# A fused attention and two-layer MoE kernel: TensorE carries the attention state on for three units instead of five, and every due offset of the planner is another

## The chip, the cores and the metric

The kernel runs on one core of a Trainium2 chip. Five engines work beside each other, each on its own list of instructions in a fixed order, and they wait for each other by semaphores: TensorE (PE in the profile; PEld is its weight loads) multiplies matrices, VectorE (DVE) and ScalarE (ACT) do elementwise work, GpSimd (POOL) too, and SyncE (SP) issues the transfers. The metric is the device time of one execution in microseconds (us).

## The reference

Three parts follow each other. The first is a recurrent attention over 4 batches, 8 heads, 768 steps and head size 48:

```python
for t in range(S):
    kt, vt, rt = (k[:, :, t], v[:, :, t], r[:, :, t])
    cur = np.einsum('bhd,bhe->bhde', u[None] * kt, vt)
    y[:, :, t] = np.einsum('bhd,bhde->bhe', rt, state + cur)
    state = w[None, :, :, None] * state + np.einsum('bhd,bhe->bhde', kt, vt)
```

Its output, 3072 tokens of 384 numbers, goes through a dense layer pair (384 to 2048 to 384, with a piecewise quadratic between). The third part picks one of eight experts for each token and applies that expert's pair of matrices (384 to 1024 to 384, relu), scaled by the gate.

## The kernel before

**Attention.** The 768 steps of a batch are cut into six units of 128 steps, so there are 24 units, u0 to u23. A unit is a few small TensorE jobs with work of the other engines between:

- `rk` (line 541, DVE) scales r and k of the unit by powers of the decay. Its input comes by a DMA into one of four buffers.
- `s0` (616, later 624, PE) makes the two 128-step score tiles of all heads; `e0` and `e1` (636, DVE) mask them out of PSUM.
- `dp` (579, PE) makes the diagonal terms from `kr` (573, POOL); `dvp` (605, DVE) multiplies them into v. From the fifth unit on this goes by `ru0`, `ru1` (566, 568, POOL), a reduction `dg2` (589, DVE) and `dv` (605, POOL).
- `s1` (694 and 690, PE) makes the unit's output; it reads dv, the masked scores and the state that the unit before left. `s3h` (748, ACT) and `s3l` (754, DVE) split the output into a rounded part xh and the rest xl.
- `s2` (PE) adds the unit's keys times values to the state. There are two ways, and `by_pe(u)`, that is `u < BY_PE` (line 674), picks one. By TensorE: one matmul with the identity brings the old state (128x384, line 715) into PSUM and eight matmuls of 48x48 (720) add to it, and ScalarE scales the sum into the new state in four instructions (680). By VectorE: sixteen smaller matmuls (724) make only the new part, VectorE adds the old state in two instructions (735; 737 where a batch begins), and ScalarE scales that in four (743).

**First layer.** Groups of nine matmuls `h` (lines 341 to 343, three products of rounded parts and rests) make 128 hidden features for 512 tokens. The first four groups, k0 to k3, take 256 tokens each: k0 and k1 need the outputs of u0 and u1. ScalarE does `relu`, `over` and `sqr` (835, 839, 842), VectorE `max` (845), ScalarE `gh` (849), GpSimd `gl` (854), and six matmuls `o` (876, 877) with three more `og` (879) add the features to the output. Before that, each 768-column piece of the weights, which come as 64-bit numbers, is put together on VectorE: pieces w0 and w1 with `wp1` to `wp3` and `wlp` (439, 442, 445, 461, two instructions each), the others with `wb1` to `wb3` (417, 420, 423) and `wlo` on POOL (481). Piece w0 is the first of the input matrix (k0 needs it), w1 the first of the output matrix, w2 the second of the input matrix; w2 is loaded first, and w1 and w0 later.

**Second layer.** It has the same shape with other names (psm, psh2, o2) and follows when the first is done.

**What sets the order.** Nothing of this order is written by hand. Each job above is a task with an engine, a planned duration, the tasks it needs, the buffers it takes and a due time. `Schedule.run` (line 111) goes through planned time, and of the tasks that could start first on an engine it takes the one with the smallest due time. To each due time, `Schedule.add` adds up to three numbers of the table `SHIFT` (line 239), found by the kind of task, by the unit or step, and by both together. The engines' instructions are then recorded in the planned order, so that table is the order. Where TensorE is planned to be idle before the first `o`, `keep_warm` (line 759) records matmuls on constants, called fillers here, of 128x128 as many as fit the planned gap (line 1719); they write a PSUM tile that nobody reads.

Two things off the path matter here. `wkr` (line 670, ACT) overwrites the second half of the table wk and so waits until `kk` (550, POOL) has read it for u2 to u7; `kk` of a unit reads that unit's keys in natural order (attn), which SP loads. And the four buffers for the units' inputs come free only with the unit's `s1`: the input of u7 waits for the end of `s1` of u3, and SP, which issues in order, issues the natural keys of u7 behind it.

Of the kernel before, what the change touches and what calls it, by code (L numbers as in the profile page):

```python
# [234 lines left out]
def d_pe(n):  # L235
    return n / 2300 + 0.011


SHIFT = {"": 31.25, "az": 14, "b0": -19.75, "b1": -26, "b2": 4.5, "b3": 22.75, "b4": -30.5, "b5": 295.25, "dd":
# [15 lines left out]
         "le0": -5.75, "le1": -39.25, "le2": -6.75, "lka": 9.25, "lkl": -20.5, "lkm": -9.5, "look": -248.5, "max":  # L255
# [14 lines left out]
         46.25, "sm": 330, "sma": -190, "smc0": -63.25, "smc1": 0.25, "sqa": -87.25, "sqs": -32.25, "swd": -3.5,  # L270
# [8 lines left out]
         "whp": 6.5, "wkc": -2.75, "wkd": -3.25, "wkr": 6.75, "wl": 109.75, "wlo": 201.5, "wlp": -72.5, "wp1": 25.25,  # L279
         "wp2": 35.25, "wp3": 54.5, "x1ld": 28.75, "x2h": 30.5, "x2l": 36, "x2ld": -14.25, "xth0": -21, "xth1": 8,  # L280
         "xtl0": -57.75, "xtl1": -6.25, "xts0": -46.5, "xts1": -3.5, "xts2": -54.75, "xts3": 7.25, "z": 98.5, "zs":
         -119.75}
U_DVE, U_PE, W_DVE = 4.7, 3.5, 4.0
ON_DVE = {}
KK_PE, W_PSUM, G_PSUM, DV_PSUM, BY_PE = 2, 2, 0, 4, 5


@with_exitstack
def fused_kernel(ctx, tc, att, wcol, wrow, ub, ucol, win, wout, emb, tau, w1, w2, out):
# [987 lines left out]
    def m2_store(b, i, o):  # L1277
# [5 lines left out]
                    "a": 2, "gh": 3, "gl": 3, "ru": 1, "dg": 2, "dv": 1, "at0": 1, "at1": 1, "state": 2, "kk": 2, "hw": 2, "gate": 1},  # L1283
                   {"PE": 5.5, "DVE": 5.75, "Pool": 4.4, "ACT": 2.2, "SP": 1.73}, SHIFT)
    parts = ((0, 0, 6), (1, 0, 8), (0, 6, NF), (1, 8, NF))
# [668 lines left out]
```

## Time and profile before

| what | value |
|---|---|
| median of 3 runs | 710.27 us (709.94 to 710.44) |
| the profiled execution | 710.95 us |
| its span, from the first to the last instruction | 709.1 us |
| TensorE busy | 699.4 us (99%) |
| VectorE busy | 450.4 us (64%) |
| ScalarE busy | 416.7 us (59%) |
| GpSimd busy | 304.8 us (43%) |

The span is 1.85 us shorter than the execution's own time, and that execution took 0.68 us more than the median. In slices of 18 us, the profile's page has TensorE at nine tenths or more everywhere but in the first (8) and the last (7), and VectorE at seven tenths or more only until about 200 us. A matmul's record ends by a model and overlaps the next one, so steps on TensorE are read from one start to the next.

### The profile page before, as it was taken

How to read it: one execution, taken by the hardware profiler on the slowest of the kernel's cores; microseconds unless marked ns; L12 is line 12 of the kernel's file. 1: busy time of each engine (PE TensorE's matmuls, PEld its weight loads, DVE VectorE, ACT ScalarE, POOL GpSimd, SP SyncE). 2: the span in 40 equal slices, each digit the busy share in tenths (PEclk: the TensorE clock that was granted, in tenths of full speed). 3: DMA queues.
4: the chain of work that ended last, by engine and by line, in shares of the span. 5: the costliest groups of instructions: out<-in, count | busy, mean ns of one | idle time of the engine just before them, and what ended most of it. 6: DMA issues, size and time to landing. Idle time of an engine off the chain costs nothing.

```text
span 709.1 us, 14241 instructions
## 1 busy us (share of the span) xinstructions
PE 699.4 (99%) x5743; PEld 597.2 (84%) x5743; DVE 450.4 (64%) x842; ACT 416.7 (59%) x744; POOL 304.8 (43%) x251
## 2 busy tenths in 40 slices
PE   8999999999999999999999999999999999999997
PEld 7788888877888888887787888887899999999996
DVE  7989987699998313235994512121588586948664
ACT  3357777566556557765756866676566364625432
POOL 4699996574476522333622322234561121112100
PEclk9999999999999999999999999999999999999999
DMA  7866445254455105322642302000412021102011
GB/s 261 321 207 209 175 155 175 67 169 161 154 176 179 65 1 177 111 91 89 221 154 86 94 0 90 1 0 1 152 35 81 3 90 44 47 0 90 6 41 48
DMA packets 26136, 74.93 MB, mean 106 GB/s; under 512 B 2505, under 2 KB 9682, under 8 KB 26066
## 3 DMA queue, kind: packets, MB, share of 16 engines
q1 hardware_dynamic: 25778, 73.59, 30.8%
q8 instruction: 46, 0.75, 0.5%
q10 hardware_dynamic: 288, 0.39, 0.2%
q14 instruction: 24, 0.20, 0.1%
HBM read 62.74 MB, written 11.01 MB: 104 GB/s over the span
## 4 chain that ended last, share of the span: by engine, by line
PE 89%; DVE 4%; POOL 2%; DMA 2%; issue 1%; ACT 1%; POOLq 0%; DVEq 0%; SPq 0%
PE psh L341 9%; PE psh L343 9%; PE psh L342 9%; PE acc L876 9%; PE acc L879 9%; PE acc L877 9%; PE o L1246 5%; PE o L1243 5%; PE o L1244 5%; PE psm L341 4%; PE psm L342 4%; PE psm L343 4%; PE psy L690 3%; DMA attn<-att 2%; PE psa L624 2%; PE pslt L1009 1%
## 5 line engine op out<-in xcount | busy, mean ns | idle before, releaser
L854 POOL TENSOR_TENSOR gl<-a,gh 128x512 fp32r<-128x512 f32 (+1 forms) x98 | 136.8, 1397 | 185.5 <-ACT gh L849 171.5
L845 DVE TENSOR_TENSOR a<-psh,a 128x512 f32<-128x512 f32 (+1 forms) x98 | 66.5, 679 | 148.3 <-ACT a L842 146.5
L876 PE MATMUL acc<-gh,wout_h 128*128 128x512 f32 (+1 forms) x294 | 116.5, 398 | 0.1
L341 PE MATMUL psh<-xh,win_h 128*128 128x512 f32 (+1 forms) x294 | 115.6, 393 | 0.0
L343 PE MATMUL psh<-xh,win_l 128*128 128x512 f32 (+1 forms) x294 | 114.9, 391 | 0.0
L342 PE MATMUL psh<-xl,win_h 128*128 128x512 f32 (+1 forms) x294 | 114.9, 391 | 0.0
L877 PE MATMUL acc<-gh,wout_l 128*128 128x512 f32 (+1 forms) x294 | 114.5, 391 | 0.0
L835 ACT ACTIVATE a<-psh,half 128x512 f32<-128x512 f32 (+1 forms) x98 | 66.3, 676 | 73.1 <-PE psh L343 64.7
L849 ACT ACTIVATE gh<-a 128x512 fp32r<-128x512 f32 (+1 forms) x98 | 60.6, 620 | 42.4 <-DVE a L845 38.4
L1203 DVE TENSOR_TENSOR sc<-sc,psm 128x256 f32<-128x256 f32 x176 | 64.1, 417 | 30.5 <-PE psm L343 20.4
L879 PE MATMUL acc<-gl,wout_h 128*128 128x512 f32 (+1 forms) x294 | 82.3, 393 | 0.2 <-POOL gl L854 0.2
L876 PEld LDWEIGHTS acc<-gh,wout_h 128*128 128x128 f32 x294 | 55.2, 188 | 15.0 <-ACT a L842 1.0
L341 PEld LDWEIGHTS psh<-xh,win_h 128*128 128x128 f32 x294 | 55.2, 188 | 13.0 <-issue 0.2
L343 PEld LDWEIGHTS psh<-xh,win_l 128*128 128x128 f32 x294 | 55.2, 188 | 12.8
L342 PEld LDWEIGHTS psh<-xl,win_h 128*128 128x128 f32 x294 | 55.2, 188 | 12.5
L879 PEld LDWEIGHTS acc<-gl,wout_h 128*128 128x128 f32 x294 | 54.3, 188 | 13.3 <-POOL gl L854 0.4
L877 PEld LDWEIGHTS acc<-gh,wout_l 128*128 128x128 f32 x294 | 55.3, 188 | 11.9
L1243 PE MATMUL o<-w2h,gh 128*128 128x384 f32 x192 | 64.6, 336 | 0.0
L1244 PE MATMUL o<-w2l,gh 128*128 128x384 f32 x192 | 64.4, 336 | 0.0
L839 ACT ACTIVATE a<-a 128x512 f32<-128x512 f32 (+1 forms) x98 | 60.9, 621 | 2.5
L842 ACT ACTIVATE a<-a 128x512 f32<-128x512 f32 (+1 forms) x98 | 60.7, 619 | 2.2
L1218 ACT ACTIVATE gh<-sc 128x512 fp32r<-128x512 f32 x44 | 26.7, 627 | 47.2 <-DVE sc L1203 43.7
(218 smaller groups left out, 1387.3 us busy)
## 6 DMA issues: line engine op xcount, KB each, us to landing
att<-att SPq DMA_DIRECT2D x22, 736.0 KB, 5.1
w<-win SPq DMA_DIRECT2D x16, 768.0 KB, 5.2
w<-wout SPq DMA_DIRECT2D x16, 768.0 KB, 4.5
attn<-att SPq DMA_DIRECT2D x20, 384.0 KB, 3.9
x1d<-x SPq DMA_DIRECT2D x6, 768.0 KB, 4.8
x1f<-x1d SPq DMA_DIRECT2D x6, 768.0 KB, 5.8
out<-o SPq DMA_DIRECT2D x10, 384.0 KB, 2.9
hw<-w SPq DMA_DIRECT2D x8, 384.0 KB, 4.0
```

Of the source, the lines that this page charges most:

```text
L341: nc.tensor.matmul(o, lhsT=sh, rhs=mh, start=first, stop=False, skip_group_check=True)
L342: nc.tensor.matmul(o, lhsT=sh, rhs=ml, start=False, stop=False, skip_group_check=True)
L343: nc.tensor.matmul(o, lhsT=sl, rhs=mh, start=False, stop=last, skip_group_check=True)
L835: nc.scalar.activation(out=a, in_=hp, func=AF.Relu, bias=half[:, 0:1], scale=0.5)
L845: nc.vector.tensor_tensor(out=a if out is None else out, in0=hp, in1=a, op=ALU.max)
L854: (eng or nc.gpsimd).tensor_tensor(out=gl, in0=a, in1=gh.bitcast(F32), op=ALU.subtract)
L876: nc.tensor.matmul(o, lhsT=wh, rhs=gh, start=(f == f0 and c0 == 0), stop=False, skip_group_check=True)
L877: nc.tensor.matmul(o, lhsT=wl, rhs=gh, start=False, stop=False, skip_group_check=True)
L879: nc.tensor.matmul(o, lhsT=wh, rhs=gl, start=False, stop=(f == f1 - 1), skip_group_check=True)
L1203: nc.vector.tensor_tensor(out=out, in0=x, in1=bank[:, j], op=op)
L1243: nc.tensor.matmul(o, lhsT=gh[:, c], rhs=ws[2][:, f, :], start=(f == 0), stop=False, skip_group_check=True)
L1244: nc.tensor.matmul(o, lhsT=gh[:, c], rhs=ws[3][:, f, :], start=False, stop=False, skip_group_check=True)
```

## The change

One constant goes from 5 to 3, so that u3 and u4 take the VectorE way of `s2`, and the table of due offsets is another one throughout. No function changes. Line numbers in the new file are one lower behind the table.

```diff
-SHIFT = {"": 31.25, "az": 14, "b0": -19.75, "b1": -26, "b2": 4.5, "b3": 22.75, "b4": -30.5, "b5": 295.25, "dd":
...
+SHIFT = {"": -15, "az": 50.75, "b0": -25.5, "b1": 9.75, "b2": 11, "b3": 27.25, "b4": 29.5, "b5": 226.5, "dd": 52.75,
...
-KK_PE, W_PSUM, G_PSUM, DV_PSUM, BY_PE = 2, 2, 0, 4, 5
+KK_PE, W_PSUM, G_PSUM, DV_PSUM, BY_PE = 2, 2, 0, 4, 3
```

The first place is VectorE near the start, from the masking of u0 (at0) to that of u1 (at1). w64_155 is the raw piece w2, w64_160 is w1, att_147, att_152 and att_157 are u0, u1 and u2. Before:

```order
L605 TENSOR_TENSOR dv_222<-att_147,psdg_202 128x256
L605 TENSOR_TENSOR dv_222<-att_147,psdg_202 128x128
L417 TENSOR_SCALAR sc_225<-w64_155 128x768
L420 SCALAR_TENSOR_TENSOR sc_225<-w64_155,sc_225 128x768
L541 TENSOR_TENSOR att_157<-att_157,pwt_112 128x1024
L423 SCALAR_TENSOR_TENSOR sc_225<-w64_155,sc_225 128x768
L754 TENSOR_TENSOR xl_239<-psy_240,xh_238 128x3x128
L605 TENSOR_TENSOR dv_289<-att_152,psdg_264 128x256
L605 TENSOR_TENSOR dv_289<-att_152,psdg_264 128x128
L439 TENSOR_SCALAR psw_293<-w64_160 128x384
L439 TENSOR_SCALAR psw_294<-w64_160 128x384
```

Now (att_158 is u2, att_276 is u3; the rows begin behind w2's three steps):

```order
L635 TENSOR_TENSOR at1_131<-psa0_235,mask_71 128x512
L635 TENSOR_TENSOR at1_131<-psa1_236,mask_71 128x512
L438 TENSOR_SCALAR psw_290<-w64_160 128x384
L438 TENSOR_SCALAR psw_291<-w64_160 128x384
L753 TENSOR_TENSOR xl_253<-psy_254,xh_252 128x3x128
L604 TENSOR_TENSOR dv_308<-att_152,psdg_278 128x256
L604 TENSOR_TENSOR dv_308<-att_152,psdg_278 128x128
L441 SCALAR_TENSOR_TENSOR psw_290<-w64_160,psw_290 128x384
L441 SCALAR_TENSOR_TENSOR psw_291<-w64_160,psw_291 128x384
L444 SCALAR_TENSOR_TENSOR psw_290<-w64_160,psw_290 128x384
L444 SCALAR_TENSOR_TENSOR psw_291<-w64_160,psw_291 128x384
L540 TENSOR_TENSOR att_158<-att_158,pwt_112 128x1024
```

The diagonal terms of u1 (dv from att_152) stood ahead of w1's first step and stand behind it now, and `rk` of u2 (att), which stood inside w2's steps, stands behind all three steps of w1.

The second place is TensorE at the outputs of u2 and u3, where state_133 and state_132 take turns. In the new order:

```order
L578 MATMUL psdg<-uw,kr 128x2 x4
L760 MATMUL wu<-mask,ident 128x128 x7
L693 MATMUL psy<-ident,dv 128x128 x3
L689 MATMUL psy<-att,state_133 32x128 x12
L689 MATMUL psy<-at_130,att 32x128 x16
L723 MATMUL pskv<-att,kk 32x48
...
L578 MATMUL psdg<-uw,kr 128x2 x4
L760 MATMUL wu<-mask,ident 128x128 x4
L693 MATMUL psy<-ident,dv 128x128 x3
L689 MATMUL psy<-att,state_132 32x128 x12
L689 MATMUL psy<-at_131,att 32x128 x16
```

Seven and four fillers (wu) stand ahead of the outputs of u2 and u3, where the order before has none, and the state of u3 is made by the sixteen small matmuls (the first is shown).

The third place is ScalarE around the first groups of the first layer; a and gh are the activations of k0, k1 and k2. Before:

```order
L835 ACTIVATE a<-psh,half 128x256
L839 ACTIVATE a<-a 128x256
L842 ACTIVATE a<-a 128x256
L849 ACTIVATE gh<-a 128x256
L670 ACTIVATE wk<-wkt 128x192
L835 ACTIVATE a<-psh,half 128x256
L839 ACTIVATE a<-a 128x256
L842 ACTIVATE a<-a 128x256
```

Now:

```order
L834 ACTIVATE a<-psh,half 128x256
L742 ACTIVATE state_132<-state_132,pwt 128x96 x4
L838 ACTIVATE a<-a 128x256
L841 ACTIVATE a<-a 128x256
L669 ACTIVATE wk<-wkt 128x192
L834 ACTIVATE a<-psh,half 128x256
L838 ACTIVATE a<-a 128x256
L841 ACTIVATE a<-a 128x256
L747 ACTIVATE xh<-psy 128x3x128
L848 ACTIVATE gh<-a 128x256 x2
```

The step gh of k0 stood ahead of `wkr` (wk from wkt); now it stands behind `wkr`, the three steps of k1 and the split of u4.

## Rows read from the trace of the kernel before

**Rows 1.** Windows of the whole program: busy us (instructions) by engine, TensorE clock, DMA.

```profile
140.00:160.00 20.00, 19.68 (x297) 15.80 (x296) 19.27 (x32) 11.43 (x22) 15.84 (x12) 1.00 0.49 155
...
sum 709.10, PE 699.37 PEld 597.22 DVE 450.37 ACT 416.73 POOL 304.77; mean PE 24.12 PEld 20.59 DVE 15.53 ACT 14.37 POOL 10.51
```

**Rows 2.** Timeline of TensorE, 11 to 64 us: start, us, line, what; idle before.

```profile
14.49 0.89 PE L715 MATMUL pskv<-state,ident 128*128 128x384 f32 x2
...
15.81 1.16 PE L616 MATMUL psa<-att 64*128 64x128 f32 x16
16.90 1.05 PE L579 MATMUL psdg<-uw,kr 128*128 128x2 f32 x8
17.88 1.16 PE L616 MATMUL psa<-att 64*128 64x128 f32 x16
19.73 0.55 PE L694 MATMUL psy<-ident,dv 128*128 128x128 f32 x3 [0.68 <-DVE at L636]
...
21.87 0.91 PE L715 MATMUL pskv<-state,ident 128*128 128x384 f32 x2
...
26.00 0.52 PE L694 MATMUL psy<-ident,dv 128*128 128x128 f32 x3
...
29.45 0.55 PE L694 MATMUL psy<-ident,dv 128*128 128x128 f32 x3
...
37.60 0.39 PE L341 MATMUL psh<-xh,win_h 128*128 128x256 f32 x1
...
46.52 0.52 PE L724 MATMUL pskv<-att,kk 128*32 128x48 f32 x32
```

**Rows 3.** Timeline of VectorE, 0 to 60 us, the stretch that starts with w1.

```profile
17.13 1.02 DVE L439 TENSOR_SCALAR psw<-w 128x384 uint32<-128x384 uint32 x2 [0.83 <-DMA w<-wout]
18.06 1.02 DVE L442 SCALAR_TENSOR_TENSOR psw<-w,psw 128x384 uint32<-128x384 uint32 x2
18.98 1.28 DVE L636 TENSOR_TENSOR at<-psa,mask 128x512 f32<-128x512 f32 x2
20.18 1.02 DVE L445 SCALAR_TENSOR_TENSOR psw<-w,psw 128x384 uint32<-128x384 uint32 x2
21.11 1.28 DVE L636 TENSOR_TENSOR at<-psa,mask 128x512 f32<-128x512 f32 x2
22.30 1.22 DVE L541 TENSOR_TENSOR att<-att,pwt 128x1024 f32<-128x1024 f32 x1
23.44 0.62 DVE L605 TENSOR_TENSOR dv<-att,psdg 128x256 f32<-128x256 f32 x2
23.96 0.56 DVE L754 TENSOR_TENSOR xl<-psy,xh 128x384 fp32r<-128x384 f32 x1
24.43 1.02 DVE L461 TENSOR_TENSOR wout_l<-psw,wout_h 128x384 fp32r<-128x384 f32 x2
```

**Rows 4.** Timeline of TensorE, 2 to 14 us: the fillers at the start.

```profile
2.02 4.16 PE L761 MATMUL wu<-mask,ident 128*128 128x128 f32 x18 [2.02 <-POOL mask L486]
...
6.46 1.50 PE L761 MATMUL wu<-mask,ident 128*128 128x128 f32 x12
```

**Rows 5.** Groups of VectorE instructions over the span: count, busy us, mean ns of one.

```profile
L589 DVE TENSOR_REDUCE dg<-ru 128x8 f32<-128x384 f32 x20 | 10.9, 547 | 0.8 <-POOL ru L568 0.2
...
L735 DVE TENSOR_TENSOR state<-pskv,state 48x192 f32<-48x192 f32 x24 | 8.4, 351 | 6.2 <-PE pskv L724 4.4 <-ACT state L743 1.5
```

**Rows 6.** Timeline of ScalarE, 0 to 60 us: `wkr` and the step of k1 behind it.

```profile
43.03 0.36 ACT L670 ACTIVATE wk<-wkt 128x192 f32<-128x192 f32 x1 [1.06 <-DMA attn<-att]
43.43 0.47 ACT L835 ACTIVATE a<-psh,half 128x256 f32<-128x256 f32 x1
```

**Rows 7.** Timeline of GpSimd, 0 to 60 us: `kk` of u7.

```profile
41.98 1.02 POOL L550 TENSOR_TENSOR kk<-attn,wk 128x384 f32<-128x384 f32 x1
```

**Rows 8.** DMA issues of the page: count, KB each, median us to landing.

```profile
att<-att SPq DMA_DIRECT2D x22, 736.0 KB, 5.1
...
attn<-att SPq DMA_DIRECT2D x20, 384.0 KB, 3.9
```

More of the change, by code (lines that the diff above doesn't have):

```diff
@@ L236, in d_pe @@
     return n / 2300 + 0.011
-SHIFT = {"": 31.25, "az": 14, "b0": -19.75, "b1": -26, "b2": 4.5, "b3": 22.75, "b4": -30.5, "b5": 295.25, "dd":
[15 rows of a table removed]
-         "le0": -5.75, "le1": -39.25, "le2": -6.75, "lka": 9.25, "lkl": -20.5, "lkm": -9.5, "look": -248.5, "max":
[14 rows of a table removed]
-         46.25, "sm": 330, "sma": -190, "smc0": -63.25, "smc1": 0.25, "sqa": -87.25, "sqs": -32.25, "swd": -3.5,
[8 rows of a table removed]
[L279 to L282, printed above, removed]
+SHIFT = {"": -15, "az": 50.75, "b0": -25.5, "b1": 9.75, "b2": 11, "b3": 27.25, "b4": 29.5, "b5": 226.5, "dd": 52.75,
[15 rows of a table added]
+         "le2": 60.25, "lka": 19.25, "lkl": 32.5, "look": -277.25, "max": -187.75, "mixl": 30.25, "o": 79, "o2": 3,
[14 rows of a table added]
+         -48.25, "sqr": 37.5, "swd": -32.5, "swh": -60.5, "swl": 16.75, "sws0": -6.25, "sws1": -25.25, "sws2": -26,
[7 rows of a table added]
+         -148.75, "wb2": -2.75, "wb3": -446.5, "whi": 20.75, "whp": -5.25, "wkc": 2.25, "wkd": -5.25, "wkr": 4.5,
[3 rows of a table added]
 U_DVE, U_PE, W_DVE = 4.7, 3.5, 4.0
 ON_DVE = {}
-KK_PE, W_PSUM, G_PSUM, DV_PSUM, BY_PE = 2, 2, 0, 4, 5
+KK_PE, W_PSUM, G_PSUM, DV_PSUM, BY_PE = 2, 2, 0, 4, 3
 @with_exitstack
```

76 rows, old and new, of the table SHIFT are left out of this document.

## The prediction

> **What bounds the kernel now.** I read the windows first: TensorE is busy for 699.37 of 709.10 us, at a clock of 1.00, and in the window from 140 to 160 us, where it misses more than in any other of 20 us behind the start, that is 0.32 us [rows 1]. The time is therefore TensorE's work plus the little that it waits, and a change of order can only change the waits. Then the timeline of TensorE from 11 to 64 us: before the first layer's first group at 37.60 it waits for single instructions of VectorE (0.68 us at 19.73) [rows 2]. Last the timeline of VectorE over the same stretch: its records follow each other without a gap, but for 0.83 us in which it waits for the weights w1, which land at 17.1 [rows 3]. So the start is VectorE's: what stands where in its list decides when TensorE may go on, and a wait of TensorE there is never made up for, since it has work for every later moment.
>
> **What the constant is worth.** The state update by TensorE takes 1.32 us (from 14.49 to 15.81), that by VectorE's way 0.52 [rows 2]. Two units: 2 x 0.80 = 1.6 us less work on TensorE. VectorE gets two additions of 0.35 us for each of the two units [rows 5], in the stretch where it has no gap; ScalarE's four scalings stay. If nothing else moved, TensorE would end 1.6 us earlier, less what the two additions delay. Everything else is the order.
>
> **The order at the start, step by step.** Durations are from one start to the next.
>
> *Output of u1.* TensorE reached this point in the kernel before at 19.73 - 0.68 = 19.05. Now the diagonal terms (0.98, from 16.90 to 17.88) and the scores (1.09, from 15.81 to 16.90) of u2 come later [rows 2], so it is there at 17.0; the diagonal of u0 now stands behind two steps of w2 and may add up to 0.5, I take 0.3. It needs the diagonal of u1 from VectorE, and that now stands behind w1's first step. VectorE was at w1 at 17.13 - 0.83 = 16.30; it has one scaling (1.14), one split (0.47) and one diagonal (0.52) less ahead of it and the masks of u1 (1.20) more [rows 3], so it comes at 15.4 and idles 1.7 us until w1 is there, twice as long as before. The loads ahead of w1 are the same ones, so I keep 17.13. Then w1's first step 0.93, a split 0.47, the diagonal 0.52: 19.05. TensorE starts 0.15 behind such an instruction (the first mask ends at 18.98 + 0.60 = 19.58, TensorE starts at 19.73 [rows 2, 3]): 19.2. The wait is 1.9 us instead of 0.68, and the start is 0.5 us earlier than before with 2.07 us less done.
>
> *Output of u2.* VectorE from 19.05: two steps of w1 (0.92, 0.93), two scalings (2.28), a split (0.47), w1's rest (0.93), four masks (2.40), the diagonal of u2 (0.52): 8.45, so 27.5 [rows 3], and TensorE may start at 27.65. TensorE's own work from 19.2: output of u1 2.14, state 1.32, two scores 2.18, diagonal 0.98 [rows 2], which is 25.8, and then seven fillers, each two records of 0.11 to 0.125 (twelve take 1.50) [rows 4]: 27.4 to 27.6. The fillers cost nothing, since VectorE is not ready either; if it were, they would cost 1.6 us by themselves. Start 27.7; before it was 26.00 [rows 2].
>
> *Output of u3.* TensorE: 27.7 + 2.14 + 0.52 + 0.98 + four fillers 0.95 = 32.3. VectorE from 27.5: w0's load now stands behind one more load of 384 KB; I take 0.2 us of waiting (between none and 1.3: a load of 736 KB takes 5.1 from issue to landing and one of 384 KB 3.9, so 352 KB more take 1.2 [rows 8]; nearer to none, since VectorE comes for it at 27.5, where before it came at about the same time). Then w0's first step 0.93, a reduction 0.47 (0.55 with the overlap of two records), two more steps 1.85, a split 0.47, the new addition of the state 0.70, the diagonal 0.52 [rows 3, 5]: 32.65. TensorE starts at 32.8; before at 29.45 [rows 2].
>
> *First group of the first layer.* 32.8 + 2.14, scores of u4 1.09, state of u4 0.52: 36.6, one us earlier than 37.60 [rows 2]. But the kernel before had done the output of u4 (2.14) and the scores of u5 (1.09) by then, and the new one has not. At equal work it stands at 36.6 + 3.2 = 39.8 against 37.6: 2.2 us behind, with the 1.6 us of the constant already in it.
>
> *First groups through ScalarE.* The step gh of k0 is now behind `wkr`. That waits for `kk` of u7 (it started right as that ended, at 43.0 [rows 6, 7]), which waits for u7's keys. Their load is issued behind the input of u7, and this waits for the end of the output of u3: 34.95. The input's 736 KB land some 5.1 us after issue [rows 8], so 40.1; the keys, by the same measure, up to 1.3 later. Then `kk` 1.02 and `wkr` 0.40: 41.5 to 42.8. Behind it are four steps of 0.45 (three of k1, a split) and gh itself, 2.2 in all (the first is 0.47 [rows 6]); the first output group may start at 43.9 to 45.2. TensorE is there at 36.6 + 2.2 (two groups) + 2.14 + 1.09 + 1.1 = 43.1, with 0.15 for a mask of u4 43.3. A wait of 0.6 to 1.9; I take 1.1, none of it there before.
>
> **Behind 60 us** the work is the same and so is the number of places at which TensorE passes from the first layer's matmuls to the attention's and back. From below a gain of 1 us is to be had (9.73 us of idle time in the span, of which 2.02 at its start [rows 4], 0.68 at 19.73, 0.32 in that window, and most of the rest behind the last matmul); from above I bound a loss by two or three waits of the size seen, 0.7 us each [rows 2]: 2 us. VectorE and GpSimd run 2 to 3 us later against the weights, but so does TensorE. I take nothing.
>
> **Sum.** 2.2 + 1.1 = 3.3 us more than the profiled 710.95, which is 709.10 us of span and 1.85 around it: 714.25. That execution was 0.68 above the median of 710.27, so against the median 713.6; I say 713.7, with 0.1 for the second state addition in front of the masks of u4.
>
> A remark on the clock. The same filler takes 0.23 us a record at the start (eighteen in 4.16) and 0.125 from 6.46 on [rows 4]: the two levels of 1.2 and 2.4 GHz, with TensorE idle before the first. The waits of up to 0.7 us later left the steps as short as ever, and so does the granted clock of 1.00 [rows 1]. The Trainium skill ("TensorE: Matmul & The Clock Gate", Part 1) says that throttled is the default state and activity releases it; by that rule the new wait of 1.9 us at the output of u1, which has no filler, could put TensorE back to the lower level, and the 6.6 us of work up to the output of u2 would take up to 6.6 more, of which VectorE's 27.5 hides only 1.8: 718. No row here shows a fall after a wait this short, so I give it 2 in 100, inside the third case below.
>
> **The rivals.**
> - *The waits don't come (no change or faster).* The order assumes w1 earlier than it lands. If it were there by 15.4, the diagonal of u1 would be done at 17.3, that of u2 at 25.8, and the outputs of u2 and u3 would start at about 26.0 and 31.1; at equal work the kernel would be 0.5 behind, the keys of u7 would come 1.7 us earlier and the wait at gh of k0 would be gone. That is 710.8, or 709.8 to 710.8 with the late waits gone. For: the fillers, which the planner only puts where it sees a gap, stand behind this point and not at it. Against: nothing in the loads ahead of w1 is less. 12 in 100 within 0.2%. To be faster, both waits and the late ones must go: 710.27 - 1.6 + 0.3 less 0.5 to 1, some 708.2. 6 in 100.
> - *Weights become late too (slower still).* The buffers of the fourth and fifth unit now go to other pieces first, and the pieces that were loaded at 38 us come later. VectorE then waits for a load while TensorE has two or three groups in hand, some 4 us; from the point where the lag passes that, each us late is one us of the end. With 2 us, the bound above: 715.7, with the clock's fall up to 718. 15 in 100.
> - *As forecast*, 713.7: 67 in 100, with its own range 712.0 to 715.2 (the first step between 0.5 less and the wait of w0 at its 1.3, the wait at gh between 0.6 and 1.9).
>
> **How the numbers follow.** A measurement of this kernel tells about 0.2% (1.4 us) from no change, so faster is below 708.85 and slower above 711.69. The forecast and the third case are both slower: 82 in 100; within 12, faster 6. The range that leaves out 2 in 10 goes from the upper end of the no-change case, 710.9, to 716.4.
>
> **What would show it.** In the profile after: VectorE's wait for w1 grows to some 1.7 us; TensorE's longest wait is at the output of u1 and ends with a diagonal term of VectorE, 1.5 us or more; the outputs of u2 and u3 start near 27.7 and 32.8, the first layer at 36.6, and TensorE waits at the first output group for gh of k0, which starts right behind a chain that `wkr` began. From 65 us on the timelines of both kernels keep their distance. It would be wrong if the output of u1 starts before 18.5, or if the distance at 65 us is made up or doubled later.

## The result, and the profile after

| kernel | median, us | ratio to the kernel before | 95% interval |
|---|---|---|---|
| before (4 runs beside it) | 710.34 (709.94 to 710.44) | 1 | |
| changed (4 runs) | 716.72 (715.08 to 717.80) | 1.0089 | 1.0069 to 1.0109 |

The change makes the kernel slower by 6.4 us. The forecast of 713.7 had the direction, but the time lies 0.3 above the upper end of its range, 716.4. The profiled execution took 716.82 us, its span is 715.0, 5.9 more than before.

TensorE's timeline of the changed kernel (start, us, line; in brackets the idle time before it and what ended it) answers to [rows 2]:

```profile
18.06 0.55 PE L693 MATMUL psy<-ident,dv 128*128 128x128 f32 x3
...
24.85 1.81 PE L760 MATMUL wu<-mask,ident 128*128 128x128 f32 x14
26.50 0.55 PE L693 MATMUL psy<-ident,dv 128*128 128x128 f32 x3
...
31.51 0.55 PE L693 MATMUL psy<-ident,dv 128*128 128x128 f32 x3
...
35.38 0.39 PE L340 MATMUL psh<-xh,win_h 128*128 128x256 f32 x1
...
45.02 0.42 PE L875 MATMUL acc<-gh,wout_h 128*128 128x256 f32 x1 [2.44 <-ACT gh L848]
45.24 0.41 PE L876 MATMUL acc<-gh,wout_l 128*128 128x256 f32 x1
...
46.43 2.08 PE L615 MATMUL psa<-att 64*128 64x128 f32 x16
```

The outputs of u1, u2, u3 and the first layer's first group start 1.1 to 1.3 us earlier than forecast. Then comes one long wait, 2.44 us at the first output group. The records behind it are slow: sixteen score matmuls take 2.08 us where they took 1.16 [rows 2]. Windows of the changed kernel over that place (busy us of each engine, and third from the end TensorE's granted clock, 1.00 being 2.4 GHz and 0.50 being 1.2):

```profile
40.00:42.00 2.00, 2.00 (x30) 1.73 (x23) 1.61 (x3) 0.00 (x0) 1.46 (x1) 1.00 0.84 206
42.00:44.00 2.00, 0.57 (x5) 0.37 (x4) 0.00 (x0) 1.39 (x4) 2.00 (x4) 1.00 0.77 280
44.00:46.00 2.00, 0.98 (x5) 0.99 (x6) 1.69 (x4) 1.27 (x4) 1.99 (x4) 0.81 0.21 86
46.00:48.00 2.00, 2.00 (x17) 1.78 (x17) 0.44 (x1) 1.31 (x3) 0.76 (x2) 0.50 0.72 201
48.00:50.00 2.00, 2.00 (x23) 1.61 (x24) 1.45 (x3) 0.00 (x0) 0.23 (x1) 0.84 0.00 0
```

TensorE is nearly idle for two windows, and then runs about four us at the lower level. In the kernel before the same windows are at 1.00 with 2.00 busy, two of them here:

```profile
44.00:46.00 2.00, 2.00 (x50) 1.75 (x49) 1.26 (x3) 1.94 (x6) 0.97 (x1) 1.00 0.04 12
46.00:48.00 2.00, 2.00 (x68) 1.93 (x58) 1.80 (x4) 1.37 (x4) 2.00 (x2) 1.00 0.23 37
```

What made gh late, on GpSimd and then ScalarE of the changed kernel (it answers to [rows 6, 7]):

```profile
40.55 1.94 POOL L549 TENSOR_TENSOR kk<-attn,wk 128x384 f32<-128x384 f32 x1 [1.99 <-DMA attn<-att]
```

```profile
42.52 0.36 ACT L669 ACTIVATE wk<-wkt 128x192 f32<-128x192 f32 x1 [3.47 <-POOL kk L549]
...
44.56 0.71 ACT L848 ACTIVATE gh<-a 128x256 fp32r<-128x256 f32 x2
```

ScalarE stands 3.47 us at `wkr`, which waits for `kk` of u7, which waits 1.99 us for its keys: the chain of the forecast's fourth step. Waits of TensorE in the changed kernel, whole span (total us, times, longest):

```profile
PE acc L875 <- ACT gh L848: 2.4, 1, 2.4
PE wu L760 <- POOL mask L485: 2.0, 1, 2.0
PE psa L623 <- issue: 0.6, 1, 0.6
...
```

The second is the wait ahead of the very first filler, which the kernel before has too [rows 4]; behind it none but the one at gh is longer than the 0.6 of the third line.

**Where the 5.9 us are.** For each stretch I added up, over all matmuls, the time from one start to the next less the median of that form (its line and shape), and then the fillers (8.53 against 5.34 us) and the work that the constant saves (1.89 by these medians), both of which fall before 42 us. Changed less before: up to 42 us +1.45; 42 to 50 us +4.24 (2.44 of it the wait, the other 1.8 put down to the slow records; compared matmul by matmul they cost 1.4, as e4 shows below); 50 to 60 us -0.59, since waits of the kernel before are not there; behind 60 us +0.74; behind the last matmul +0.1. With another choice of a form's usual step, neighbouring stretches trade some 0.3 us.

### The profile page after: what moved, and what is told of

Its sections match the earlier page's. It is cut to its first block, busy times and chain, and to the rows that moved or that the text cites. A ratio compares the mean times of both kernels' runs of the same rounds, so it can differ in the third digit from the quotient of the medians.

```text
span 715.0 us, 14340 instructions
## 1 busy us (share of the span) xinstructions
PE 703.5 (98%) x5793; PEld 601.5 (84%) x5793; DVE 452.1 (63%) x846; ACT 415.3 (58%) x744; POOL 304.9 (43%) x251
## 4 chain that ended last, share of the span: by engine, by line
PE 91%; DVE 3%; POOL 1%; ACT 1%; issue 1%; DMA 1%; POOLq 0%; DVEq 0%; ACTq 0%
PE acc L875 10%; PE psh L340 9%; PE acc L878 9%; PE acc L876 9%; PE psh L341 9%; PE psh L342 9%; PE o L1245 5%; PE o L1242 5%; PE o L1243 5%; PE psm L340 4%; PE psm L341 4%; PE psm L342 4%; PE psy L689 4%; PE psa L623 2%; PE psa L615 1%
```

## The experiments

In e1 and e8, theory A is that the first output group's wait, and the clock's fall behind it, are what the forecast lacked, and theory B that the order lags everywhere; the other runs name their own. The kernels are made from the changed one, or from the one before, by moving tasks in the planned list; the kernel before, run beside them, had medians of 710.49 to 710.71.

```diff
-    for task in sch.run():
+    todo = sch.run()
+    def ahead(kind, item, kind2, item2):    # puts the first task right ahead of the second
+        at = lambda a, b: next(n for n, t in enumerate(todo) if (t.kind, t.item) == (a, b))
+        task = todo.pop(at(kind, item))
+        todo.insert(at(kind2, item2), task)
+    for task in todo:
```

| run | made from | median, us | ratio to before | 95% interval |
|---|---|---|---|---|
| e1 keys of u7 first | changed | 715.29 (714.02 to 716.60) | 1.0058 | 1.0039 to 1.0076 |
| e2 fillers at the output group | changed | 715.43 (715.19 to 716.36) | 1.0066 | 1.0045 to 1.0086 |
| e3 no fillers | changed | 716.32 (715.80 to 717.36) | 1.0079 | 1.0058 to 1.0101 |
| e4 first loads as before | changed | 713.93 (713.86 to 715.82) | 1.0052 | 1.0034 to 1.0070 |
| e5 constant alone | before | 711.04 (710.74 to 712.56) | 1.0012 | 1.0003 to 1.0021 |
| e6 gh ahead of wkr | changed | 714.07 (713.31 to 715.16) | 1.0044 | 1.0029 to 1.0059 |
| e7 gh late | before | 714.47 (714.22 to 715.73) | 1.0058 | 1.0043 to 1.0073 |
| e8 e1 and e6 together | changed | 714.03 (713.67 to 715.53) | 1.0054 | 1.0039 to 1.0069 |
| e9 e7 with fillers | before | 712.67 (712.17 to 713.31) | 1.0029 | 1.0017 to 1.0041 |
| e10 e8, constant 5 | changed | 714.32 (713.22 to 715.15) | 1.0056 | 1.0040 to 1.0071 |

**One piece of the change in the kernel before (e7), and the clock by itself (e9).**

```diff
+    for task in (("kk", "u7"), ("wkr", ""), ("relu", "k1"), ("over", "k1"), ("sqr", "k1")):
+        ahead(*task, "gh", "k0")
```

> The kernel before with this one piece of the change: kk of u7, wkr and the three first steps of k1 stand ahead of gh of k0; nothing else is moved. In the kernel before the first output group starts at 42.20 without a wait, wkr starts at 43.03 right behind kk of u7. Theory A (a wait of this kind costs itself, and the clock's fall behind it as much again in part): gh of k0 at 44.8, the first output group at 45.3, a wait of 3.1 us; behind it some 4 us at a granted clock of 0.5 to 0.8, 1.7 to 2 us more; 710.5 + 5 = 715.5. Rival 1 (the wait alone, clock 1.00): 713.6. Rival 2 (waits behind it are saved, the time is made up): under 712.

The profiled run's wait, and its windows:

```profile
44.79 0.57 PE L876 MATMUL acc<-gh,wout_h 128*128 128x256 f32 x1 [2.80 <-ACT gh L849]
...
48.33 0.63 PE L879 MATMUL acc<-gl,wout_h 128*128 128x256 f32 x3
```

```profile
42.00:44.00 2.00, 0.00 (x0) 0.00 (x0) 1.39 (x3) 1.25 (x3) 0.63 (x1) 1.00 0.16 65
44.00:46.00 2.00, 1.21 (x5) 1.22 (x6) 1.29 (x2) 0.72 (x2) 1.19 (x1) 0.71 0.01 4
46.00:48.00 2.00, 2.00 (x16) 1.78 (x17) 0.00 (x0) 1.50 (x4) 1.62 (x3) 0.50 0.03 8
48.00:50.00 2.00, 2.00 (x39) 1.64 (x40) 1.29 (x2) 0.42 (x1) 2.00 (x2) 0.94 0.00 0
```

Theory A's mechanism, wait and fall, is reproduced by five tasks moved. The time alone, 714.47, lies between theory A's 715.5 and the 713.6 of a wait without a fall; the windows at 0.50 decide. The cost is 4.0 us where I wrote 5: the wait is 2.80 in place of 3.1, and 0.75 of later waits are saved between 50 and 60 us. Then the same with work of no use in the wait:

```diff
             first_o = "acc0" in [b.tag for b in task.alloc]
             if not first_o and end:
                 keep_warm(max(0, int((task.start - end - 0.35) / 0.22)))
+            if first_o:
+                keep_warm(11)
```

> The kernel before with gh of k0 late, as in the run before this, and eleven fillers (22 records, 2.6 us) on TensorE in the wait that this makes ahead of the first output group (2.80 us there, then 4 us at a granted clock of 0.50 to 0.94, 714.47 us). It prices the clock by itself in the order of the kernel before. Theory A (idle time ahead puts the clock down, work of no use keeps it up): the output group starts at 44.8 as there, the clock stays 1.00, and the 1.6 us that the slow records cost from 44.8 to 48.4 are gone: 712.8. Rival 1 (the slow records are not the clock's answer to the wait): 714.5. Rival 2 (the fillers run past gh): 0.2 to 0.4 of the gain is lost, 713.1.

```profile
42.00:44.00 2.00, 1.95 (x18) 1.76 (x16) 0.92 (x3) 1.74 (x5) 0.13 (x1) 1.00 0.05 20
44.00:46.00 2.00, 1.71 (x20) 1.58 (x22) 1.26 (x2) 0.36 (x2) 1.68 (x2) 1.00 0.05 12
46.00:48.00 2.00, 2.00 (x46) 1.71 (x46) 0.49 (x2) 1.41 (x5) 1.63 (x3) 1.00 0.00 0
```

```profile
44.29 0.39 PE L876 MATMUL acc<-gh,wout_h 128*128 128x256 f32 x1 [0.34 <-ACT gh L849]
...
46.28 0.62 PE L879 MATMUL acc<-gl,wout_h 128*128 128x256 f32 x3
```

The clock stays at 1.00, and the time is 1.8 us less (2.1 by the ratios), with intervals that just do not touch. Theory A's number was 712.8. The same matmuls, from the first of the output group to `og`, take 1.99 us here and 3.54 in e7: 1.55 is the clock's own price, and the rest of the difference is not told apart, since e9's profiled run reached the output group 0.5 us earlier. The Trainium skill ("TensorE: Matmul & The Clock Gate", Part 1) says that the throttled clock is the default and activity releases it; e7 and e9 agree.

**The same in the changed kernel (e2).** Ten fillers in place of eleven, at the same place.

> The changed kernel with ten fillers (20 records, 2.35 us) on TensorE right ahead of the first output group, where it idles 2.44 us; all else in place. It tells the wait from the clock. Theory A (the idle time put the clock down): the first output group still starts at about 45.0, since gh is no earlier, the granted clock stays 1.00 behind it, and the time is 1.9 us less, about 714.8. Rival 1 (the slow steps from 45 to 49 us are not the clock's answer to the wait): the clock falls as before, 716.7. Rival 2 (fillers end behind gh): the start moves to 45.1 to 45.4, and half a us of the gain is gone.

The clock stayed at 1.00 and 1.3 us went (1.6 by the ratios). In the profiled run the whole start was 0.9 later (the output group at 45.93, behind gh and not behind a filler), and the time alone does not tell this kernel from the changed one, as the intervals overlap. So the clock's part is shown by the windows here, and by a time only in e9.

**Taking the wait away (e1, e6, e8).** Edits: `ahead("l2", "u7", "l01", "u7")` in e1; `ahead("max", "k0", "wkr", "")` and `ahead("gh", "k0", "wkr", "")` in e6; all three in e8.

> The changed kernel with one exchange on SP: the keys of u7 (384 KB) are issued ahead of its input (736 KB). In the changed kernel the keys were issued at 34.60 us behind the input and landed at 40.41; kk of u7 (1.94), wkr, three steps of k1 and a split stood behind them, and the first output group waited 2.44 us, until 45.02. Behind it 4 us show a granted clock of 0.50 to 0.84. Theory A (this wait, and the clock that falls behind it, are the loss beyond the forecast): keys land at 37.5 to 38.5, kk of u7 starts by 39.6, the wait at the first output group is 0 to 0.3, the clock stays 1.00, and the time falls by 2.4 + 1.9 = 4.3 to about 712.4 (711.8 to 713.2). Theory B (the order lags everywhere, and what is saved here is waited for later): 715 to 716.5, with new waits behind 50 us. Theory C (the clock falls for another reason than this wait): the wait goes and the clock still falls, 714.3.

> The changed kernel with VectorE's max and ScalarE's gh of k0 ahead of wkr, as in the kernel before; wkr and the steps of k1 stay behind kk of u7. Theory A (wkr ahead of gh was what made the first output group late): gh of k0 is done by 41.2, the first output group follows H without a wait at about 42.4; the second waits for gh of k1, 0.5 to 1.1 us; no fall of the clock; 2.4 + 1.9 - 0.9 = 3.4 us less than the changed kernel: 713.3 where the loads land as in its profile. Rival (the wait goes to the second output group whole, and the clock falls there): 715.5 to 716.7.

> The changed kernel with both mends: keys of u7 issued ahead of its input, and gh of k0 ahead of wkr. Theory A: no wait at either of the first two output groups and no fall of the clock at 45 us; what is left is the start, 1.2 us behind at equal work, and 0.7 us of waits behind 60 us: 712.3 to 713.0 in runs in which GpSimd's kr of u3 does not wait for the keys of u4, 714 to 716.6 where it does (1.95 us in the profile of the run with the keys alone, with the clock's fall behind it). Theory B (the rest of the order is behind as well): never under 713.5.

In e1 the wait at the output group is gone and its windows from 40 us on are at 1.00, but the profiled run met another wait ahead of the place that was edited, with the same fall:

```profile
30.85 1.52 PE L578 MATMUL psdg<-uw,kr 128*128 128x2 f32 x8 [1.95 <-POOL kr L572]
```

```profile
30.00:32.00 2.00, 1.15 (x7) 1.15 (x8) 2.00 (x5) 0.98 (x2) 1.76 (x2) 0.81 1.01 345
32.00:38.00 6.00, 6.00 (x69) 5.10 (x69) 5.90 (x9) 1.17 (x4) 5.48 (x5) 0.50 0.27 84
```

GpSimd's `kr` of u3 is behind `kk` of u4, whose keys came at 25.80 in this run and by 23.43 in that of the changed kernel, where the wait was 0.39. So e1's time fits theory B's number by another mechanism than B's. In e6 and e8 no wait at gh of k0 is left, their clock is 1.00 from 14 to 52 us, and by the ratios 2.5 to 3.2 us of the 6.4 are back. The time of e6, 714.07, is nearer its theory A (713.3) than its rival (715.5 at least), and the wait of 0.5 to 1.1 us that was expected at the second output group is not there. But no execution of e8 came below 713.5, as theory B had said, and theory A had it at 712.3 to 713.0, since the profiled run had no long wait for the keys of u4 (0.40 at `dp` of u3): the rest, half of the 6.4 or more, is a lag that the mends don't touch. No run here takes it away; where it lies is read from the sums alone. By the sum over matmuls, e8 is 2.1 behind the kernel before at 42 us and loses 0.9 behind 60 us, in waits such as these two:

```profile
PE o L1245 <- DVE gl L1222: 0.7, 1, 0.7
...
PE psa L623 <- issue: 0.6, 1, 0.6
```

**The start (e4, e3).** In e4, `ahead("l01", "u2", "ubl", "")` and `ahead("l2", "u3", "wkd", "")`; e3 drops the call of `keep_warm` in the loop, and so also six fillers that its expectation doesn't name, the twelve records ahead of the first unit (from 6.88 in the changed kernel); the output of u1 started at 18.04 all the same.

> The changed kernel with the first loads on SP issued in the order of the kernel before: the input of u2 ahead of ubt, and the keys of u3 ahead of the two pieces of wk; VectorE and TensorE keep the new order. In the kernel before w1 landed at 17.11, in the changed one at 14.54, and the prediction had kept 17.13. Theory A (the order of the loads set that): w1 lands at about 17, VectorE idles about 1.5 us for it, the output of u1 starts at 19.2 (the prediction's number) instead of 18.06, and all behind it 1.1 later: 717.8. Rival 1 (the landing differs from run to run, or hangs on something else): w1 at 14.5 to 15, output of u1 at 18.1, 716.7.

w1 landed at 14.79 with the old order of loads, so rival 1 holds on the landing, and not on the time. By the ratios the time is 2.6 less than the changed kernel's, which no theory expected: the whole start was 0.5 earlier, the keys of u7 landed at 39.37 in place of 40.41, the wait at the output group was 0.99, and the clock did not fall:

```profile
43.04 0.39 PE L875 MATMUL acc<-gh,wout_h 128*128 128x256 f32 x1 [0.99 <-ACT gh L848]
...
45.05 0.39 PE L875 MATMUL acc<-gh,wout_h 128*128 128x256 f32 x1
```

From the first output group to the second the changed kernel takes 3.42 us (45.02 to 48.44), e4 2.01 for the same matmuls: the fall cost the changed kernel 1.4 there. Whether the order of the loads makes e4 faster, or luck of the landings, stays open: the intervals of the two kernels just overlap.

> The changed kernel without the eleven fillers ahead of the outputs of u2 (14 records from 24.85) and u3 (8 records from 30.36). Theory A (VectorE sets both starts, its diagonals end just as the fillers do; waits of 1.65 and 1.15 us do not put the clock down): both outputs start where they did, 26.5 and 31.5, clock 1.00 until the first output group, 716.7 within 0.5. Rival 1 (the fillers were the last to end): the outputs start up to 0.3 earlier each, 716.2. Rival 2 (waits as short as these put the clock down): a granted clock below 1.00 behind 26.5 or 31.5, the work up to the next output at half rate, of which VectorE hides about half: 718 to 720.

The output of u2 started where it had (26.59 in place of 26.50), so VectorE sets it and the fillers cost nothing there. But the clock fell:

```profile
26.59 0.55 PE L693 MATMUL psy<-ident,dv 128*128 128x128 f32 x3 [1.51 <-DVE dv L604]
```

```profile
26.00:28.00 2.00, 1.41 (x35) 1.27 (x39) 2.00 (x6) 0.00 (x0) 1.21 (x2) 0.97 0.39 148
28.00:38.00 10.00, 9.48 (x145) 8.35 (x137) 8.71 (x15) 2.92 (x8) 8.16 (x8) 0.50 0.43 123
```

Rival 2's mechanism at theory A's time: ten us at the lower clock, and yet 716.32, because TensorE then reached the output group later, waited 0.53 there and did not fall again.

**The constant (e5, e10).** In e5, in the kernel before, VectorE's two additions and ScalarE's scalings take the place of ScalarE's task for u3 and u4, and everything else keeps its order; e10 does the opposite on top of e8.

```diff
+    def by_pe(u):
+        return u < 3
+    for task in todo:
+        if task.kind == "s2p" and task.item in ("u3", "u4"):
+            task.fn = lambda u=int(task.item[1:]): (s2_ev(u), s2_w(u))
```

> The kernel before, in its own order, with the constant alone: the state of u3 and u4 is added by VectorE (two additions of 0.35 us each), in the place that ScalarE's four scalings had; TensorE's work is 2 x 0.80 = 1.6 us less. Theory A (VectorE sets the starts of the outputs up to 37 us, so TensorE waits longer where it has less to do): 0.2 to 0.9 less, 709.6 to 710.3, with waits of up to 0.7 us at the diagonals of u3 and u4. Rival 1 (TensorE is the bound here too): the full 1.6 less, 708.9. Rival 2 (the two additions stand in VectorE's list ahead of masks and splits that TensorE waits for): 0.5 more, 711.2. The start up to 28 us is that of the kernel before, so its profile also shows w1's landing (17.11 in the profile before) once more: 14.5 to 15.6 if that one landing was a straggler, as in the five other profiles, 17 if it hangs on the kernel.

```profile
28.25 0.55 PE L694 MATMUL psy<-ident,dv 128*128 128x128 f32 x3 [0.56 <-DVE dv L605]
...
33.30 1.58 PE L616 MATMUL psa<-att 64*128 64x128 f32 x16 [1.27 <-issue]
```

Rival 2 came nearest: 0.55 us slower, which is within 0.2%, though the interval leaves out 1. The work that TensorE saves came back as waits (the second one ended by nothing that the profile shows).

> The changed kernel with both mends (keys of u7 first, gh of k0 ahead of wkr, 714.03 us) and the constant at its old value: TensorE adds the state of u3 and u4 again (1.6 us more work), ScalarE writes it from PSUM, and VectorE's four additions of 0.35 us are gone; the order is the changed one. Theory A (VectorE's list sets the start, so the constant took more than it gave; alone in the kernel before it cost 0.55): 713.4, 0.3 to 0.8 less than with the mends alone. Rival (TensorE's work counts in full behind the start): 715.0 to 715.6.

714.32 beside e8's 714.03: in the changed order the constant makes no difference that these runs tell, neither theory A's 0.3 to 0.8 less nor the rival's 1.0 and more. Its profiled run has the wait that I had forecast for the change: w1 landed at 16.88, and the output of u1 waited for VectorE. Behind it the clock fell, to which I had given 2 in 100.

```profile
18.76 0.60 PE L693 MATMUL psy<-ident,dv 128*128 128x128 f32 x3 [1.65 <-DVE dv L604]
```

```profile
18.00:20.00 2.00, 1.24 (x19) 0.99 (x23) 2.00 (x6) 0.26 (x2) 2.00 (x2) 0.78 0.85 289
20.00:22.00 2.00, 2.00 (x44) 1.81 (x40) 2.00 (x3) 0.96 (x2) 1.33 (x2) 0.50 1.01 418
```

I had priced that fall at up to 4.8 us (6.6 less 1.8). From there to the output of u2 it took 9.59 us (18.76 to 28.35), where it took 8.44 in the changed kernel, so this one cost 1.2 at most. In e6 w1 was late too (16.71), and behind a shorter wait the clock stayed at 1.00:

```profile
18.59 0.55 PE L693 MATMUL psy<-ident,dv 128*128 128x128 f32 x3 [1.41 <-DVE dv L604]
```

None of these ten kernels beats the kernel before.

## Why the prediction was right in direction and short in size

- **The constant.** Right as a sum that is eaten: I had 1.6 us less work inside a start that loses 2.2 all the same. What the two additions delay I had left open; e5 prices it at more than the 1.6, since VectorE, which has no gap there [rows 3], gets them.
- **Output of u1: failed in the profiled run.** I kept 17.13 for w1's landing from one execution. It was 14.54, VectorE came at 16.21 and did not wait, and the output started at 18.06, under the 18.5 that I had named as the sign of being wrong. VectorE would have come at the 15.4 that I had (16.21 - 0.80), but stood 0.80 us at the masks of u0 for scores of TensorE:

```profile
10.40 1.29 DVE L635 TENSOR_TENSOR at<-psa,mask 128x512 f32<-128x512 f32 x2 [0.80 <-PE psa L615]
...
16.21 1.01 DVE L438 TENSOR_SCALAR psw<-w 128x384 uint32<-128x384 uint32 x2
```

```profile
6.88 1.89 PE L760 MATMUL wu<-mask,ident 128*128 128x128 f32 x12
8.60 0.60 PE L554 MATMUL pskk<-ident,att 128*128 128x128 f32 x4
```

  TensorE began the first unit at 8.60, in the kernel before at 7.80: the same twelve fillers took 1.89 in place of 1.50 [rows 4]. Neither is the kernel's. TensorE began there at 7.79 in e10 and at 8.43 in e7, and over the twelve profiles of this case w1 landed at 14.5 to 15.6 in nine (15.01 in e5, whose start is that of the kernel before) and 16.71, 16.88 and 17.11 in three. In e6 (1.41) and e10 (1.65) the wait that I forecast at 1.9 is there. So the forecast rested on the rarer landing, and whether a run has the wait is chance.
- **Outputs of u2 and u3, first group.** The steps between them were right: 8.44 (forecast 8.5), 5.01 (5.1) and 3.87 (3.8). All came earlier by what the first had not lost, and the lag at 42 us was 1.45 by the sum over matmuls instead of 2.2; e8's profile has 2.1.
- **First output group: the chain was right, its wait too small.** Forecast a start at 43.9 to 45.2 and a wait of 0.6 to 1.9, taken as 1.1; it started at 45.02 after 2.44. TensorE was there 0.9 before the 43.3 that I had, again by w1, and `kk` took 1.94 for 1.02. The start's gain did not reach ScalarE's chain and became idle time: the output of u3 started 1.3 earlier than forecast, and yet the keys of u7, issued at 34.60, landed only at 40.41, inside the 40.1 to 41.4 that I had. My first rival had w1 there by 15.4, and from it the keys 1.7 us earlier, no wait, and 710.8; its condition held here, and its result did not.
- **The clock: the step that failed.** I asked only whether the wait at u1 could bring the clock down, gave it 2 in 100 because waits of up to 0.7 had not, and never put the question to the other wait that I had just forecast with an upper end of 1.9. The term that the sum put at nothing cost 1.4 us here (3.42 us against 2.01 in e4) to 1.8 (by the sum over stretches), and 1.55 between e7 and e9. Up to the output group the sum held nearly (1.45 + 2.44 = 3.9 against 3.3), though not because its terms did: 0.75 less in the first, 1.3 more in the second. The clock's fall on top took the time out of the range. At u1, where I had looked for it, it came in e10.
- **Behind 60 us.** I took nothing, with bounds of -1 and +2; it was +0.74, and between -0.1 and +1.5 in the profiles of e1 to e4. The distance was neither made up nor doubled.

## What to carry to other kernels

Price every wait that a new order makes on TensorE twice: by itself, and by the lower clock on the work behind it; where nothing earlier can be put there, work of no use in the wait gives the second part back. Take a transfer's landing from several executions before a forecast rests on it, or carry its spread in the range. A saving on an engine that waits for another one is worth what that other engine leaves of it, which one run with the saving alone tells.

## What the runs showed of the hardware

- What came behind a wait of TensorE with no filler in it, up to 52 us, in the profiles: after 2.80, 2.44, 1.95, 1.65 and 1.51 us the granted clock fell to 0.50; after 1.41 (e6), 1.27 (e5), 1.20 (e3 at 14.15) and 0.99 (e4) it stayed at 1.00. With fillers in the wait it stayed at 1.00 in e2 and e9. The windows above show the lower level until past 48 us in e7, and from 28 to 38 us in e3.
- The same loads were issued ahead of w1 in all twelve profiles, and it landed over a spread of 2.6 us. The latest and the earliest, before (issued at 5.38) and changed (5.18), with KB and us to landing:

```profile
w<-wout SPq DMA_DIRECT2D x1, 768.0 KB, 11.7
...
w<-wout SPq DMA_DIRECT2D x1, 768.0 KB, 9.4
```

  Where it was latest, the transfers of the kernel before were nearly all done already (third number from the end the clock, then the busy share of 16 DMA engines, which is about one engine's):

```profile
16.00:18.00 2.00, 2.00 (x26) 1.86 (x26) 1.17 (x4) 1.11 (x5) 2.00 (x2) 1.00 0.07 19
```

  The Trainium skill ("DMA: Bandwidth & Descriptors", Why a DMA increments its semaphore by 16 and not by 1) says that a transfer is split over up to 16 engines that finish independently and counts as landed when all have; that row agrees.
- GpSimd's `kk` took 1.94 us in the changed kernel, where it ran beside VectorE's `rk` (1.22 from 40.40), and 1.02 before [rows 7]. The Trainium skill ("GPSIMD Engine Reference", Specifications) names contention with VectorE's instructions of two SBUF inputs, of which `rk` is one; the two rows agree. No run was made for it, but in e4 and e6 `kk` of u7 started first (39.50 and 41.12) and took 1.00, and the `rk` that started 0.38 and 0.14 us behind it took 1.71 and 1.94.
